# One z row through DRAM, dummies on the constant tile and a new order table in a gated linear-attention and SwiGLU kernel

## The chip, the cores and the metric

The program runs on one core of a Trainium2 chip. The metric is the device time of one execution in microseconds (us). The profile's span, from the first to the last instruction, was 1.24 to 1.39 us shorter than the device time of the same execution, so spans and times can be compared term by term.

TensorE is called PE below, VectorE DVE, ScalarE ACT, GpSimd POOL, SyncE SP.

## The reference, cut to what matters

```python
# S = 2048 tokens, D = 640, H = 32 heads of 20, F = 1728
g = sigmoid((x * gate_w).sum(-1))
# A: linear attention
phi_q = concat[softmax(q w_phi), softmax(-q w_phi)];  phi_k likewise
kv = phi_k^T v;   z = sum over tokens of phi_k          # per head
o  = (phi_q kv) / (phi_q z + 1e-6)
a  = o @ wo
# B: SwiGLU
b  = (silu(x @ w_gate) * (x @ w_up)) @ w_down
out = g * a + (1 - g) * b
```

## The kernel before

The kernel is a list of work items in a hand-tuned order. Each item issues a piece of PE work with what follows it on ACT, DVE and POOL, and every engine runs its part in that order. The letters that matter: H is a pair of dummy matmuls, put there so that PE comes to full speed earlier (the intent); X transposes a tile of x; U and V make V tiles; M makes a part of the K weights; K, S, P, E are the stages of a K tile; N finishes kv and z; Z spreads z over all partitions; Q, A, B, C, c are the stages of a Q tile (B multiplies by the spread z); F is one 128-column piece of gate and up; O is a third of the head outputs of 512 tokens; D is a tile of the output. I cuts the ring of PSUM pairs from four to three, because two banks are then held for kv; N gives the fourth back.

```python
    def next_pair():                      # the least recently used pair of PSUM banks
        return used([r for r in ring["lru"] if r < ring["n"] and r not in held][0])

    def warm():                           # H: `ones` is filled by DVE at the start
        pr = next_pair()
        mm([(bank(2 * pr, 0, P), ones[:, :], ones[:, :], True, True, False)] * NWARM)

    def kv_finish():                      # N
        ...
        reduce(zf[0:120, :], zt[0:120, :, :])
        tt("dve", dz[0:120, :, :], ident[...] broadcast, zf[...] broadcast, ALU.mult)
        ...                               # six products that write kvsb

    def z_broadcast():                    # Z: ones^T dz puts every z on every partition
        pr = next_pair()
        dzf = dz[0:120, :, :].rearrange("p j c -> p (j c)")
        mm([(bank(2 * pr, 0, 480), ones[0:120, :], dzf[:, 0:480], True, True, False),
            (bank(2 * pr + 1, 0, 480), ones[0:120, :], dzf[:, 480:960], True, True, False)])
        copy("act", zb[:, 0:960]..., halves(pr, 480))
        ...                               # and a third matmul and copy for the last 360

    # the last store of the program, issued by ACT; the others by SP
    # at the end SP waits for all stores:
    for s, v in out_evs:
        sp.wait_ge(tr.sem[s], v)
```

The softmax here doesn't subtract the row's maximum and nothing guards it: scores larger than these inputs give would overflow.

## Time and profile before

| | before |
|---|---|
| device time, median of 3 (later 5) | 290.45 us (290.59) |
| span of the profiled run | 289.1 us |
| PE busy | 285.7 us, 99% |
| DVE, ACT, POOL busy | 57%, 51%, 56% |

From the page of the kernel before, the heading, its first part (busy us, share, instructions) and its fourth part (the chain that ended last, by engine and by line):

```profile
span 289.1 us, 4875 instructions
PE 285.7 (99%) x1975; PEld 174.5 (60%) x1975; DVE 165.3 (57%) x242; ACT 147.7 (51%) x252; POOL 160.6 (56%) x124
...
PE 99%; DVE 0%; issue 0%
PE ps L294 98%; PE ps L306 1%; DVE xT L318 0%; DVE osb L712 0%; DVE ones L340 0%
```

The same chain in order of time (start us, length us, what):

```profile
1.12 2.10 PE ps L294 x18
...
8.89 278.26 PE ps L294 x1914
287.15 0.02 issue
287.18 0.32 DVE osb L712
```

PE runs without a break from 8.89 to 287.15 us. What the change can win lies in the PE work itself, in the start, and in the 2.1 us from the start of the last matmul to the end of the span, which is one eviction and the landing of the last store. PE busy time alone doesn't show this, since the ends of matmuls are modelled; the starts do: matmuls of 512 columns follow each other every 216 ns, those of 320 columns every 136 (medians in this profile).

The timeline has the matmuls that the change removes and the O parts that it makes adjacent (start us, us, engine, line, operation, out<-in, form, count):

```profile
77.22 0.72 PE L294 MATMUL ps<-dz,ones 120*128 120x480 bf16 x3
...
121.07 0.62 PE L294 MATMUL ps<-phiT,kvsb 120*64 120x512 bf16 x4
121.63 1.25 PE L294 MATMUL ps<-xT,wg 128*128 128x512 bf16 x5
122.72 1.24 PE L294 MATMUL ps<-xT,wu 128*128 128x512 bf16 x5
123.89 1.06 PE L294 MATMUL ps<-phiT,kvsb 120*64 120x512 bf16 x7
```

The DMA view of the last 2.3 us, its instruction queue q14 and its issues (KB each, us from issue to landing); the second store is the program's last:

```profile
q14 instruction: 1, 0.01, 1.0%
issues: line engine op xcount, KB each, median us to landing
out_dram<-osb SPq DMA_DIRECT2D x1, 56.0 KB, 1.6
out_dram<-osb ACTq DMA_DIRECT2D x1, 24.0 KB, 1.5
```

These lines come back below: one packet of 8 KB on the instruction queue stands beside the last store. Here it began 1.18 us after the store's issue, when the last of the store's own packets had ended (1.12 us).

### The profile page before, as it was taken

Reading aid. Unit: us, or ns where it says so; the run is one execution under the profiler, and the core shown is the slowest. Engines: PE = TensorE matmul, PEld = TensorE weight load, DVE = VectorE, ACT = ScalarE, POOL = GpSimd, SP = SyncE. Lnnn points to the kernel's source line nnn. Section 1 sums busy time; section 2 is a strip of 40 time slices with the busy share of each in tenths; the row PEclk is TensorE's granted clock in tenths of the full one; section 3 lists DMA queues with packets and bytes.
Section 4 is the critical chain, followed back from the end, with each engine's and each line's share of the span. In section 5 each row is a group of like instructions: output and inputs, shape, how many; then the busy total and the mean of one; then the engine's idle time right before and its main releaser. Section 6 shows DMA issues by size and latency. Waiting matters only on the chain.

```text
span 289.1 us, 4875 instructions
## 1 busy us (share of the span) xinstructions
PE 285.7 (99%) x1975; PEld 174.5 (60%) x1975; DVE 165.3 (57%) x242; ACT 147.7 (51%) x252; POOL 160.6 (56%) x124
## 2 busy tenths in 40 slices
PE   8999999999999999999999999999999999999997
PEld 6667777757444545457765566556444447556776
DVE  1258586865599994679989562549633883000000
ACT  1368687856747536762364542624655551344112
POOL 8587979994447886746435544256258586111000
DMA  7966798000006852202440323030402005000101
GB/s 220 189 122 128 107 263 298 3 3 0 0 2 170 239 112 50 50 2 50 106 114 0 77 50 73 25 73 23 52 0 41 11 0 124 25 23 0 48 23 49
DMA packets 48777, 21.28 MB, mean 74 GB/s; under 512 B 39346, under 2 KB 48754, under 8 KB 48754
## 3 DMA queue, kind: packets, MB, share of 16 engines
q1 hardware_dynamic: 47368, 20.25, 30.7%
q10 hardware_dynamic: 1386, 0.71, 0.8%
q8 instruction: 16, 0.26, 0.4%
q14 instruction: 7, 0.06, 0.1%
HBM read 8.96 MB, written 2.62 MB: 40 GB/s over the span
## 4 chain that ended last, share of the span: by engine, by line
PE 99%; DVE 0%; issue 0%
PE ps L294 98%; PE ps L306 1%; DVE xT L318 0%; DVE osb L712 0%; DVE ones L340 0%
## 5 line engine op out<-in xcount | busy, mean ns | idle before, releaser
L322 POOL TENSOR_TENSOR hT<-hT,us 128x512 bf16<-128x512 bf16 (+1 forms) x56 | 69.0, 1239 | 77.7 <-DVE hT L326 77.5
L326 DVE SCALAR_TENSOR_TENSOR hT<-hT,ps 128x512 bf16<-128x512 bf16 (+1 forms) x56 | 38.0, 684 | 69.1 <-ACT hT L312 64.7
L294 PE MATMUL ps<-xT,wg 128*128 128x512 bf16 x260 | 64.6, 379 | 0.0
L294 PE MATMUL ps<-xT,wu 128*128 128x512 bf16 x260 | 64.6, 379 | 0.0
L294 PE MATMUL ps<-wd,hT 128*128 128x320 bf16 (+2 forms) x462 | 63.9, 295 | 0.0
L312 ACT ACTIVATE hT<-ps 128x512 bf16<-128x512 f32 (+2 forms) x60 | 35.8, 597 | 41.1 <-PE ps L294 40.8
L294 PEld LDWEIGHTS ps<-wd,hT 128*128 128x128 bf16 x462 | 44.5, 98 | 17.8
L322 POOL TENSOR_TENSOR ph<-eq,qc 128x1320 bf16<-128x1320 bf16 x16 | 39.3, 2456 | 16.2 <-DVE qc L625 12.4
L294 PE MATMUL ps<-wqk,xT 128*128 128x320 bf16 x320 | 47.7, 299 | 0.0
L294 PEld LDWEIGHTS ps<-xT,wu 128*128 128x128 bf16 x260 | 25.4, 98 | 30.7
L294 PEld LDWEIGHTS ps<-xT,wg 128*128 128x128 bf16 x260 | 25.1, 98 | 29.0 <-issue 1.3
L312 ACT ACTIVATE osb<-ps,omg 128x640 bf16<-128x640 f32 (+2 forms) x17 | 12.9, 757 | 57.9 <-PE ps L294 57.9
L322 POOL TENSOR_TENSOR ekr<-ekr,krec 128x1280 bf16<-128x1280 bf16 x16 | 37.3, 2357 | 4.8 <-DVE krec L336 4.7
L294 PEld LDWEIGHTS ps<-wqk,xT 128*128 128x128 bf16 x320 | 30.4, 98 | 13.4 <-issue 0.4
L312 ACT ACTIVATE us<-ps 128x512 bf16<-128x512 f32 (+1 forms) x56 | 33.4, 596 | 0.1
L312 ACT ACTIVATE eq<-ps 128x640 bf16<-128x640 f32 x32 | 22.3, 703 | 21.2 <-POOL ph L322 14.2
L333 DVE TENSOR_REDUCE ksum<-ekr 128x64 f32<-128x1280 bf16 x16 | 23.4, 1461 | 9.6 <-ACT ekr L312 9.6
L312 ACT ACTIVATE ekr<-ps 128x640 bf16<-128x640 f32 x32 | 22.3, 703 | 6.4 <-PE ps L294 5.9
L294 PE MATMUL ps<-wvg,xT 128*128 128x320 bf16 (+1 forms) x160 | 24.9, 302 | 0.3 <-DVE xT L318 0.3
L333 DVE TENSOR_REDUCE qz<-eq 128x64 f32<-128x1280 bf16 x16 | 23.6, 1478 | 2.2 <-ACT eq L312 2.2
L294 PE MATMUL ps<-wog,oT 128*128 128x320 bf16 (+2 forms) x165 | 24.7, 294 | 0.0
L333 DVE TENSOR_REDUCE qw<-ez 128x64 f32<-128x1280 bf16 x16 | 23.7, 1479 | 0.2
(73 smaller groups left out, 190.3 us busy)
## 6 DMA issues: line engine op xcount, KB each, us to landing
out_dram<-osb SPq DMA_DIRECT2D x15, 160.0 KB, 1.8
wd<-in_B_w_down_dram SPq DMA_DIRECT2D x1, 2080.0 KB, 9.7
wg<-in_B_w_gate_dram SPq DMA_DIRECT2D x1, 1040.0 KB, 10.0
wu<-in_B_w_up_dram SPq DMA_DIRECT2D x1, 1040.0 KB, 12.2
wg<-in_B_w_gate_dram SPq DMA_DIRECT2D x1, 800.0 KB, 5.5
wu<-in_B_w_up_dram SPq DMA_DIRECT2D x1, 800.0 KB, 7.7
wog<-in_A_wo_dram SPq DMA_DIRECT2D x2, 375.0 KB, 7.0
wvg<-in_A_wqkv_dram SPq DMA_DIRECT2D x4, 160.0 KB, 3.7
```

Source lines behind the costliest of these rows:

```text
L294: last = pe.matmul(o, lhsT=l, rhs=r, start=st, stop=sp_, skip_group_check=sk)
L306: last = pe.transpose(o, i, ident[0:k, 0:k])
L312: return run("act", lambda: act.activation(o, i, func, scale=scale), rd, [o])
L322: return run(e, lambda: eo.tensor_tensor(o, a, b, op), [a, b], [o])
L326: return run("dve", lambda: dve.scalar_tensor_tensor(out=o, in0=a, scalar=s, in1=b, op0=op0, op1=op1), rd, [o])
L333: return run("dve", lambda: dve.tensor_reduce(o, i, AX.X, ALU.add), [i], [o])
```

## The change

The intent: take the three z matmuls off PE (z becomes a row by one PE transpose, goes to DRAM and comes back spread over the partitions by a DMA), start the dummies without waiting for a filled tile, run the O parts of one block next to each other, and lay out the order anew around the longer way of z. The diff, cut to its core:

```diff
-H0 H1 H2 H3 H4 H5 H6 H7 H8 G X0 H9 H10 H11 U0.0 X1 U0.1 U1.0 ...
-... V3 Y i4 F0.0 F0.1 M0 V4 M2 M1 M3 i3 M4 K0 K1 S0 I P0 ...
-... E12 E13 E14 E15 Q2 Q0 Q1 N J T F0.13 F1.8 A0 F1.7 Z B1 B0 F1.12 C0 c0 B2 F1.5 F1.2 F0.8 A2 C2 L Q3 F0.4 ...
-... F0.12 B4 O0.1 F0.3 O0.0 C4 O0.2 B6 F1.4 c4 B5 Q7 ...
+H0 H1 H2 H3 H4 H5 H6 H7 H8 H12 G X0 H9 H10 H11 U0.0 X1 H13 U0.1 U1.0 ...
+... V3 Y F0.1 M1 i3 M0 I F0.0 M2 V4 M3 M4 K0 K1 S0 V6 ...
+... E13 F1.11 E14 Q1 E15 Q0 Q2 N A0 Z J F0.9 F0.13 F1.13 A1 B1 B0 F1.2 F1.3 F1.0 C0 ...
+... F0.4 A5 B4 Q6 F0.11 C4 O0.0 O0.2 c4 B5 A6 O0.1 C5 c5 Q7 Q8 B6 C6 c6 D0.1 ...
@@ on-chip tiles
-    ones = sb("ones", [P, P], BF16)
-    dz = sb("dz", [P, NCH, 120], BF16)
+    zh = sb("zh", [P, P], BF16)
+    zr = sb("zr", [P, 120], BF16)
-    memset("dve", ones[:, :], 1.0)
@@ def fills(i)
+            memset("pool", zh[:, NCH:P], 0.0)
@@ def warm()
-        mm([(bank(2 * pr, 0, P), ones[:, :], ones[:, :], True, True, False)] * NWARM)
+        c = nc.const_aps.tensor(1.0, [P, P], BF16)
+        ...  # NWARM matmuls with c as both operands
@@ def kv_finish()
-        tt("dve", dz[...], ident[...], zf[...], ALU.mult)
+        copy("dve", zh[0:120, 0:NCH], zf[0:120, :])
@@ Z
-    def z_broadcast(): ...
+    zrow = nc.dram_tensor("zrow", (NCH, 120), BF16, kind="Internal").ap()
+    def z_row():
+        pr = next_pair()
+        o = bankbf(2 * pr, 120)
+        transposes([(o, zh[0:120, :])], 120)
+        copy("act", zr[0:NCH, :], o[0:NCH, :])
+        dma("sp", zrow, zr[0:NCH, :])
+        dma("sp", zb[:, :], bass.AP(zrow.tensor, zrow.offset, [[0, P], [1, FP]]))
```

More of the change, by code (lines that the diff above doesn't have):

```diff
@@ L36 @@
 ORDER = """
-H0 H1 H2 H3 H4 H5 H6 H7 H8 G X0 H9 H10 H11 U0.0 X1 U0.1 U1.0 U1.1 X2 U0.2 U1.2 U2.0 U2.1 X3 U2.2
-U0.3 U1.3 U2.3 U0.4 U1.4 U2.4 V3 Y i4 F0.0 F0.1 M0 V4 M2 M1 M3 i3 M4 K0 K1 S0 I P0 K3 S1 K2 V6 V8
-E0 K4 S3 S2 V5 P1 P3 P2 E1 V11 S4 P4 K5 V7 E2 K6 E3 K7 S5 S6 S7 E4 R1 P5 K8 R2 P6 E5 S8 V9 K9 P7
-E6 V10 P8 K10 S9 R3 E7 K11 E8 S10 R0 K12 P9 R4 P10 S11 E9 V14 K13 P11 S12 E10 K14 P12 E11 S13 P13
-K15 S14 V12 V13 P14 S15 P15 F0.6 F0.2 V15 E12 E13 E14 E15 Q2 Q0 Q1 N J T F0.13 F1.8 A0 F1.7 Z B1
-B0 F1.12 C0 c0 B2 F1.5 F1.2 F0.8 A2 C2 L Q3 F0.4 c2 A1 F1.13 F0.5 F1.6 C1 F1.1 Q5 F1.0 A3 F1.10 B3
-c1 Q4 C3 F1.9 c3 F0.7 F0.10 Q6 F0.11 F1.3 A4 F0.9 F0.12 B4 O0.1 F0.3 O0.0 C4 O0.2 B6 F1.4 c4 B5 Q7
-A6 A5 C5 c5 C6 D0.1 A7 c6 B7 C7 Q8 D0.2 D0.0 c7 A8 Q9 A9 B9 C9 Q10 F1.11 B8 c9 D0.3 C8 O1.1 B10
-A10 O1.0 O1.2 F2.6 c8 Q12 F2.3 Q11 F2.7 F2.1 B11 D1.0 C10 c10 F2.2 D1.1 A11 F2.4 Q13 C11 c11 F2.5
-A12 B13 D1.3 F2.13 F2.0 B12 C12 D1.2 A13 O2.0 O2.1 O2.2 C13 Q14 A14 c12 F2.10 F3.11 F2.12 F3.9
-F3.6 F2.9 B14 c13 Q15 F2.11 F2.8 F3.7 C14 F3.10 F3.0 B15 F3.13 A15 F3.3 F3.4 c14 C15 c15 F3.12
-F3.8 D2.2 D2.3 F3.1 F3.2 D2.0 O3.0 O3.1 O3.2 F3.5 D2.1 D3.1 D3.0 D3.2 D3.3
+H0 H1 H2 H3 H4 H5 H6 H7 H8 H12 G X0 H9 H10 H11 U0.0 X1 H13 U0.1 U1.0 U1.1 X2 U0.2 U1.2 U2.0 U2.1
+X3 U2.2 U0.3 U1.3 U2.3 U0.4 U1.4 U2.4 V3 Y F0.1 M1 i3 M0 I F0.0 M2 V4 M3 M4 K0 K1 S0 V6 V5 S1 P0
+K3 K2 P1 E0 V9 K4 E1 S3 V7 P3 K5 S2 V8 V10 S4 P2 P4 E2 R0 E3 K6 S5 P5 S6 i4 E4 V14 K7 K8 P6 V15 S7
+R2 E5 K9 S8 P7 R1 E6 K10 S9 V12 P8 E7 P9 K11 S10 P10 F0.8 R3 F1.10 E8 E9 K12 E10 S11 S12 K14 S14
+V11 K13 P11 P12 E11 K15 P14 R4 S13 P13 F1.9 S15 P15 E12 V13 T F1.8 E13 F1.11 E14 Q1 E15 Q0 Q2 N A0
+Z J F0.9 F0.13 F1.13 A1 B1 B0 F1.2 F1.3 F1.0 C0 c0 B2 F0.3 F1.12 A2 C2 F0.2 F0.7 F0.12 L c2 Q3 A3
+F1.6 C1 B3 c1 F1.4 F1.1 F1.7 F0.6 Q4 C3 c3 A4 F1.5 F0.5 F0.10 Q5 F0.4 A5 B4 Q6 F0.11 C4 O0.0 O0.2
+c4 B5 A6 O0.1 C5 c5 Q7 Q8 B6 C6 c6 D0.1 B7 Q9 D0.3 A7 C7 c7 D0.0 B9 A9 Q10 B8 D0.2 C9 O1.2 O1.0 c9
+O1.1 A8 F2.3 F2.8 Q12 F2.10 A12 F2.4 F2.13 A10 C8 c8 F2.6 F2.7 Q11 F2.0 B11 A11 B10 C11 c11 D1.0
+C10 B12 c10 F2.9 D1.2 D1.3 D1.1 O2.2 C12 O2.1 O2.0 F3.13 F2.12 F3.10 c12 F3.11 Q15 F2.1 F2.11 Q13
+Q14 F2.2 A15 F3.1 A14 B13 F3.6 F3.7 B14 A13 F3.0 F3.8 C13 F2.5 C14 c14 F3.3 c13 F3.12 B15 F3.9
+D2.3 C15 c15 F3.2 F3.5 D2.2 D2.0 O3.2 O3.0 O3.1 F3.4 D2.1 D3.2 D3.1 D3.0 D3.3
 """
@@ L466, in warm, with fn @@
         pr = next_pair()
-        mm([(bank(2 * pr, 0, P), ones[:, :], ones[:, :], True, True, False)] * NWARM)
+        c = nc.const_aps.tensor(1.0, [P, P], BF16)
+        def fn():
+            for _ in range(NWARM):
+                last = pe.matmul(bank(2 * pr, 0, P), lhsT=c, rhs=c, start=True, stop=True)
+            return last
+        run("pe", fn, [], [bank(2 * pr, 0, P)])
     def v_pairs(t, pr):
@@ L568, in kv_finish @@
         reduce(zf[0:120, :], zt[0:120, :, :])
-        tt("dve", dz[0:120, :, :], ident[0:120, 0:120].unsqueeze(1).to_broadcast([120, NCH, 120]),
-           zf[0:120, :].unsqueeze(2).to_broadcast([120, NCH, 120]), ALU.mult)
+        copy("dve", zh[0:120, 0:NCH], zf[0:120, :])
         for bk, j0, j1 in ((KV0, 0, 8), (KV0 + 1, 8, NCH)):
@@ L576, in kv_finish @@
                    hmask[0:120, hh:hh + 1].unsqueeze(1).to_broadcast([120, n, DH]), ALU.mult)
-    def z_broadcast():
+    zrow = nc.dram_tensor("zrow", (NCH, 120), BF16, kind="Internal").ap()
+    tr.reg(zrow.tensor, "sbuf", 1 << 20)
+    def z_row():
         pr = next_pair()
-        dzf = dz[0:120, :, :].rearrange("p j c -> p (j c)")
-        mm([(bank(2 * pr, 0, 480), ones[0:120, :], dzf[:, 0:480], True, True, False),
-            (bank(2 * pr + 1, 0, 480), ones[0:120, :], dzf[:, 480:960], True, True, False)])
-        copy("act", zb[:, 0:960].rearrange("p (b c) -> p b c", b=2), halves(pr, 480))
-        pr = next_pair()
-        mm([(bank(2 * pr, 0, 360), ones[0:120, :], dzf[:, 960:FP], True, True, False)])
-        copy("act", zb[:, 960:FP], bank(2 * pr, 0, 360))
+        o = bankbf(2 * pr, 120)
[3 more added lines that the diff above has]
+        dma("sp", zb[:, :], bass.AP(zrow.tensor, zrow.offset, [[0, P], [1, FP]]))
     def gates():
@@ L730, in _build @@
         "f": lambda i: load_ffn(FCUT[i], FCUT[i + 1]), "L": load_late_weights, "T": tail_weights, "J": gates,
-        "Y": w_blocks, "I": kv_begin, "N": kv_end, "Z": z_broadcast,
+        "Y": w_blocks, "I": kv_begin, "N": kv_end, "Z": z_row,
         "Q": qtile, "A": qsum, "B": qden, "C": qscale, "c": qmul,
```

## The prediction

> **What bounds the kernel.** TensorE. The page gives PE 285.7 of 289.1 us busy; the chain of waits is 99% PE, 278 us of it unbroken from 8.9 us. Busy is not peak, so I compared matmul starts in the timeline: 512-column matmuls start every 216 ns[...]. Another 1.1 us lies before the first matmul, 2 us after the last. DVE (57%), ACT (51%) and POOL (56%) have slack. No reordering can win 2% (5.8 us).
>
> **On PE.**
> - z: three matmuls against `ones` (0.56 us from start to next start) go, one 120-column transpose (0.05 us) comes: -0.5 us.
> - O parts: entering and leaving a run of O matmuls costs about 95 ns each. The first block has two runs (121.1 and 123.9 us), now one: -0.2 us.
> - Dummies: without the memset (0.90 to 1.07 us) the first can start 0.2 us earlier, but the first transposes wait for x0, landing at 3.17 us. H12 fills this time, H13 sits in the wait for the second xT copy. 0 to -0.25 us[...].
>
> **Off PE.** DVE loses the 1.53 us dz product, ACT 1.34 us of zb evictions. The z row takes two dependent DMAs: about 2 us to DRAM (stores here land in 1.77 us[...])[...]. With the copy behind the exponentials of three Q items, zb should land 7 to 8 us after the transpose (before: 2.5 from the z matmuls). Three F items, A0 and A1 lie between; DVE should wait 0 to 2 us at the first zb product. That costs nothing: four PSUM pairs hold PE's next items.
>
> **The new order.** I walked it by hand with the trace's durations (F 2.16 us, K/Q/V 1.36, E 0.34; POOL: kmul 2.36, hT 1.15, ph 2.43). In the K phase POOL gains 3.6 us (fill of ph) and 2 us (hT of F0.8, F1.10), but PE gains the F time too, and each E item finds its kmul 1 to 2 us early. M1 starts near 14.1 us, after its wT (11.6 us). phiT lands 5 us ahead of the first O block. So I expect no PE stall over 0.3 us after 9 us: the order re-covers a PE that was covered.
>
> **Time.** 290.45 - 0.5 - 0.2 - 0.1 = 289.65 us; range 288.8 to 290.8, the upper side for an overlooked stall. Faster by over 2%: 0.01; within 2%: 0.96; slower: 0.03.
>
> **What would show it.** Right: span near 288.3 us, chain still 98 to 99% PE; z matmuls replaced by one transpose; one O run per block; the DVE wait on zb now released by a DMA, up to 2 us, no PE gap beside it; first matmul near 0.93 us and first transposes of x still near 3.2 us. Wrong: PE gaps near 40 to 75 us (E items waiting for POOL), at the first M items, or after the z row; or the x transposes moving.
>
> **What would make it wrong.** The zb chain taking over 12 us, so that DVE holds all four PSUM pairs; POOL falling behind in the K phase[...].

The sum under "Time": 290.45 - 0.5 (z) - 0.2 (O parts) - 0.1 (dummies) = 289.65 us. The 0.1 was the estimate within the 0 to -0.25 us. The 7 to 8 us for zb stand as the estimate. From the trace of before: the medians of the time from each matmul's start to the next, taken by shape and tiles, add up to 283.9 of the 285.8 us between the first and the last start, and of the other 2.0 us 1.6 lie before 8.9 us.

## The result

The changed kernel took 291.62 us (median of 5, 291.38 to 291.81), the kernel before 290.59 us (median of 5, 289.97 to 290.79). The ratio is 1.0038, 95% interval 1.0023 to 1.0052: 1.1 us slower where 0.8 us faster was expected.

The page of the changed kernel has the same shape, but its chain is no longer all PE:

```profile
span 290.4 us, 4891 instructions
PE 284.9 (98%) x1977; PEld 174.6 (60%) x1977; DVE 162.9 (56%) x241; ACT 147.5 (51%) x251; POOL 160.4 (55%) x125
...
PE 96%; DMA 2%; DVE 1%; SPq 0%; ACT 0%; issue 0%
```

Its chain in order of time:

```profile
1.73 4.95 DMA wvg<-in_A_wqkv_dram
...
6.72 1.00 PE ps L294 x6
...
17.87 0.61 ACT hT L312
18.48 0.02 issue
18.50 0.69 DVE hT L326
19.19 0.74 DVE wqk L318
19.93 0.14 issue
20.07 59.32 PE ps L294 x562
...
129.46 0.08 issue
129.54 158.03 PE ps L294 x1020
287.57 0.02 issue
287.59 0.32 DVE osb L718
```

The PE stream now has three interruptions: a wait for weights at 6.72 us, one for a DVE copy (line L318, `wqk`) at 20.07 us, a short one at 129.54 us. The timeline shows that the two intended savings on PE took place: one transpose in place of three matmuls, and one run of O parts:

```profile
79.22 0.22 PE L306 MATMUL ps<-ident,zh 120*128 120x120 bf16 x1
...
127.97 1.49 PE L294 MATMUL ps<-phiT,kvsb 120*64 120x512 bf16 x11
129.54 2.88 PE L294 MATMUL ps<-wqk,xT 128*128 128x320 bf16 x20
```

The DMA view of the last 3.2 us:

```profile
q14 instruction: 1, 0.01, 1.0%
issues: line engine op xcount, KB each, median us to landing
out_dram<-osb SPq DMA_DIRECT2D x1, 56.0 KB, 1.6
out_dram<-osb ACTq DMA_DIRECT2D x1, 24.0 KB, 2.4
```

The last store takes 2.4 us to land, 0.9 more than before, with the same bytes.

One pair of profiles is a thin basis. Both kernels were therefore profiled a second time, and every later kernel gives one profile more. The table splits each span, by matmul starts in the trace, into the start (to the first F matmul), the stream (first F to the last matmul's start; the stretch to the first K matmul is given apart) and the end.

| kernel | start | F to K | stream | end | last store lands after | SP instructions |
|---|---|---|---|---|---|---|
| before | 12.03 | 7.43 | 274.90 | 2.13 | 1.49 | 82 |
| b_again | 13.99 | 7.43 | 274.91 | 2.09 | 1.45 | 82 |
| b_const | 11.58 | 7.43 | 274.91 | 2.13 | 1.49 | 82 |
| b_wait2 | 12.05 | 7.43 | 274.92 | 2.11 | 1.47 | 82 |
| b_order | 12.11 | 7.66 | 275.81 | 2.09 | 1.45 | 82 |
| b_sp2 | 12.67 | 7.43 | 274.90 | 3.02 | 2.38 | 84 |
| b_dma2 | 11.96 | 7.43 | 274.91 | 2.97 | 2.16 | 84 |
| after | 12.72 | 7.66 | 274.63 | 3.02 | 2.38 | 84 |
| a_again | 12.14 | 7.66 | 274.63 | 2.91 | 2.27 | 84 |
| a_ones | 11.99 | 7.66 | 274.89 | 2.89 | 2.26 | 84 |
| a_wait12 | 12.37 | 7.66 | 274.62 | 2.93 | 2.30 | 84 |
| a_oldorder | 12.27 | 7.43 | 277.31 | 2.92 | 2.28 | 84 |
| a_f12 | 12.19 | 7.65 | 274.62 | 2.09 | 1.45 | 82 |
| a_latei | 11.88 | 7.27 | 274.41 | 3.08 | 2.44 | 84 |
| a_best | 11.52 | 7.26 | 274.41 | 2.18 | 1.54 | 82 |

Where the code of the stream is the same, the stream repeats to 0.02 us, but for a_ones (below). The end is 2.09 to 2.18 us in one group of kernels and 2.89 to 3.08 us in the other, with nothing between. The start differs from run to run. (a_best3, the last kernel, is not in the table: start 14.29, F to K 7.27, stream 278.93, end 2.17, last store 1.52, 82 SP instructions.) So from the changed code comes -0.28 us of stream and +0.85 us of end (means of the two profiles each), together +0.57 us. Neither the waits of the PE view alone nor one pair of spans would have told this.

### The profile page after: what moved, and what is told of

It is laid out like the page before. It is cut to its first block, busy times and chain, and to the rows that moved or that the text cites. A ratio compares the mean times of both kernels' runs of the same rounds, so it can differ in the third digit from the quotient of the medians.

```text
span 290.4 us, 4891 instructions
## 1 busy us (share of the span) xinstructions
PE 284.9 (98%) x1977; PEld 174.6 (60%) x1977; DVE 162.9 (56%) x241; ACT 147.5 (51%) x251; POOL 160.4 (55%) x125
## 4 chain that ended last, share of the span: by engine, by line
PE 96%; DMA 2%; DVE 1%; SPq 0%; ACT 0%; issue 0%
PE ps L294 96%; DMA wvg<-in_A_wqkv_dram 2%; SPq L348 0%; DVE wqk L318 0%; DVE hT L326 0%; PE ps L306 0%; ACT hT L312 0%; DVE osb L718 0%
## 5 line engine op out<-in xcount | busy, mean ns | idle before, releaser
L322 POOL TENSOR_TENSOR hT<-hT,us 128x512 bf16<-128x512 bf16 (+1 forms) x56 | 65.6, 1181 | 68.0 <-DVE hT L326 67.8
L322 POOL TENSOR_TENSOR ph<-eq,qc 128x1320 bf16<-128x1320 bf16 x16 | 42.3, 2645 | 26.1 <-DVE qc L631 24.0
L312 ACT ACTIVATE eq<-ps 128x640 bf16<-128x640 f32 x32 | 22.4, 704 | 17.3 <-POOL ph L322 10.4
L333 DVE TENSOR_REDUCE ksum<-ekr 128x64 f32<-128x1280 bf16 x16 | 23.5, 1470 | 10.4 <-ACT ekr L312 10.4
```

What stands on the lines that cost most here:

```text
L312: return run("act", lambda: act.activation(o, i, func, scale=scale), rd, [o])
L322: return run(e, lambda: eo.tensor_tensor(o, a, b, op), [a, b], [o])
L333: return run("dve", lambda: dve.tensor_reduce(o, i, AX.X, ALU.add), [i], [o])
```

## The experiments

### Is the slow start the change's?

The first suspicion was the start: in the first profile of the changed kernel the second chunk of the V weights landed at 6.68 us instead of 5.17, and U0.1 waited 1.4 us for it. Theory 1: the change does this. Theory 2: landing times are chance. Four runs: both kernels unchanged, before with the constant-tile dummies alone (`b_const`), and after with the filled tile back (`a_ones`).

```diff
# b_const, against before (ones and its memset stay, for z)
-        mm([(bank(2 * pr, 0, P), ones[:, :], ones[:, :], True, True, False)] * NWARM)
+        c = nc.const_aps.tensor(1.0, [P, P], BF16)
+        ...  # as in the changed kernel
# a_ones, against after: the same the other way round, with
+    ones = sb("ones", [P, P], BF16)
+    memset("dve", ones[:, :], 1.0)
```

> The kernel before, unchanged, for a second profile. Theory 1 (the changed kernel's start is slower by itself): the second w chunk of the V weights lands again near 5.2 us, the second x transposes are followed by U items at 6.3 us, the last store lands 1.5 us after its issue; time 290.5 us. Theory 2 (landing times of the first loads and of the last store are chance of each execution): the chunk lands anywhere between 5 and 7 us and the last store takes 1.5 to 2.4 us, with the time following them.

> The changed kernel, unchanged, for a second profile. Theory 1: the second w chunk lands again near 6.7 us with a PE gap of about 1.4 us before U0.1, and the last store takes 2.4 us again; 291.6 us. Theory 2: this profile shows a landing near 5.2 us or a short last store, and then a span near 289 us, though the five times before were all 291.4 to 291.8.

> The kernel before with only the dummies reading the constant tile (the ones tile and its memset stay, for z). If the earlier and differently placed dummies disturb the first loads: U0.1 or U1.0 waits for the second w chunk near 6.7 us and the time is 0.7 us above before. If not: first matmul at 0.84 us instead of 1.12[...], time within 0.3 us of before or 0.2 faster.

> The changed kernel with the dummies reading a filled tile again, all else as changed (also puts 256 bytes per partition back, so every later tile moves). If the constant-tile dummies are the cause of the slow start: 0.7 us faster than the changed kernel, 290.9 us. If the order, the z row or chance is: 291.6 us as before it.

Measured: b_again 291.07 us (289.92 to 292.36), a_again 291.48 us (290.93 to 292.95), b_const 290.62 us, a_ones 291.13 us, beside 290.37 us for before on that chip (289.86 to 293.32). The spans of the second pair of profiles have the opposite sign of the first: before 291.0, after 289.7 us. In the timeline of PE in b_again, the kernel before, stands a wait for the same DMA as in the changed one. The first profile of the kernel before, which has no such wait:

```profile
6.30 0.72 PE L294 MATMUL ps<-wvg,xT 128*128 128x320 bf16 x4 [0.31 <-DVE xT L318]
```

The first profile of the changed kernel:

```profile
6.72 1.00 PE L294 MATMUL ps<-wvg,xT 128*128 128x320 bf16 x6 [1.40 <-DMA wvg<-in_A_wqkv_dram]
```

And b_again:

```profile
5.08 0.74 PE L306 MATMUL ps<-ident,xs 128*128 128x128 bf16 x5
6.63 1.79 PE L294 MATMUL ps<-wvg,xT 128*128 128x320 bf16 x6 [0.81 <-DMA wvg<-in_A_wqkv_dram]
```

The chunk landed at 5.2, 6.6, 5.3, 5.5, 5.5, 6.1 and 5.5 us in the seven profiles of kernels made from before, and at 6.7, 6.1, 5.4, 5.3, 5.4, 5.1, 5.2 and 5.4 in the eight of the table made from after. Theory 1 falls as far as the landings go: either code has early and late ones. The time of a_ones, 291.13 us, lies between its two expectations (290.9 and 291.6) and decides nothing. The constant tile does what it was meant to in one respect (first matmul at 0.84 us instead of 1.12), but the PE then waits for the same DMAs.

The landing is not all of the scatter. The six matmuls above take 1.79 us in b_again and 1.00 us in the changed kernel: in b_again they start 240 to 270 ns apart, in the changed kernel 135 to 147. So PE was still at about half speed in b_again. By the spacing of its matmuls (at 128 columns 107 ns before and 56 ns after in the kernel before) PE came to full speed at 4.1 to 10.0 us in the seven profiles with dummies on the filled tile (5.5 us in before, 10.0 in b_again), and at 3.9 to 10.4 us in the nine with the constant tile (4.1 us in after, 10.4 in a_best3). The two slowest starts, 13.99 us (b_again) and 14.29 us (a_best3), are the two in which PE came to full speed last. So the earlier dummies do not fix the time of full speed, and what they win, if anything, is below the scatter of the start.

(The 0.26 us by which the stream of a_ones is longer than that of after is a wait at F0.8 near 52.3 us: the last up weights landed at 52.2 us in that run, at 50.8 and 51.6 us in the two profiles of the changed kernel. The new order asks for them that early.)

### Where does the late last store come from?

In the packet records of the trace, one DMA packet of 8 KB on an instruction queue (0.46 to 0.61 us long) falls beside the last store in every profile; the expectations call it the fetch. In the kernel before it began 1.18 us after the store's issue, when the store's own packets (0.86 to 1.12 us) were done. In the changed kernel it began 1.02 us after the issue, lasted 0.58 us, and the last of the store's packets ended only 0.1 us after it: 1.70 us after the issue. None of the store's own packets took over 24 ns; some started late. The trace shows two instruction queues, q8 with packets of 16 KB and q14, that of this packet, with packets of up to 8 KB; it does not name the engine whose instructions a packet holds. The packet lies right before the late store packets (1.59 to 1.69 us). But whose is it, and why does it lie there only in the changed kernel? Theory F: it is ScalarE's, and its place goes with ScalarE's instructions, 300 here instead of 298. Rivals: the order, the z row, the memory layout.

```diff
# b_wait2: two semaphore instructions more on ACT (four satisfied waits), before the 14th output
# a_wait12: twelve more, against after
+        if t == 13:
+            for _ in range(4):            # 24 in a_wait12
+                act.wait_ge(tr.sem["pe"], 1)
# b_order: before with the order table of after;  a_oldorder: after with the order table of before
```

> The kernel before plus two ScalarE semaphore instructions that are already satisfied (300 instructions instead of 298), placed where ScalarE waits 4 us for matmuls. Theory F (ScalarE's fetch of its next 8 KB of instructions[...] collides with that store's packets in the changed kernel because ScalarE has 300 instructions there): the fetch starts about 1.02 us after the last store's issue instead of 1.17, the store takes 2.3 us instead of 1.5, from last matmul start to the end of the span 2.9 us instead of 2.1, all else as before; about 0.8 us slower. Rival (the late last store comes from the new order, the z row or memory layout): 2.1 us at the end, no change.

> The changed kernel plus twelve satisfied ScalarE semaphore instructions (312). Theory F: the last 8 KB fetch starts 0.8 to 1 us earlier against the store's issue and is out of the way of its packets: last store 1.5 us, end 2.1 us after the last matmul start instead of 2.9; about 0.8 us faster than the changed kernel. Rival: end stays at 2.9 us.

> The new order with everything else as before (z by three matmuls, dummies on the filled tile). From the first F matmul to the last matmul start, 274.90 us in the kernel before and 274.63 in the changed one: here 275.1 if the z row is worth 0.5 us of it and the order costs 0.2 (wait at the M items 0.39 instead of 0.17, wait after the adjacent O parts eating their gain). If instead the z row brought waits of its own: below 274.6. ScalarE has 301 instructions here and SyncE as many as before: by theory F the last store is late or near to it, by the rivals z row or layout it is not.

> The changed kernel with the old order table. zb lands about 6 us after the z transpose, VectorE waits 4 to 5 us for it at the first product. Theory 1 (four PSUM pairs cover this): no PE gap over 0.1 us beside it, 274.4 us from the first F to the last matmul start, so the z row did not need the new order. Theory 2 (the order had to be redone for the longer z path): PE gaps of 1 us or more at the F and Q items after the z transpose. ScalarE has 297 instructions here and SyncE 84 as in the changed kernel: theory F says last store 1.5 us, end 2.1 us.

Measured: b_wait2 290.75, a_wait12 291.64, b_order 291.62, a_oldorder 294.68 us, beside 290.91 for before. The ends in the table: 2.11, 2.93, 2.09 and 2.92 us. Theory F falls on all four: ScalarE's count is 300, 312, 301 and 297, and the end does not follow it. The order is not it either: b_order has the new order and the short end, a_oldorder the old one and the long end. What goes with the long end is the z row, or SP's two instructions more (84 instead of 82) that issue its DMAs. Three theories remained (SP's instructions, the number of DMAs, the layout of on-chip memory), told apart by two further kernels made from before and one made from after:

```diff
# b_sp2, against before: as b_wait2, on SP (two semaphore instructions more)
+                sp.wait_ge(tr.sem["pe"], 1)
# b_dma2, against before: two tiny DMAs of SP to a spare row in DRAM, waited for by DVE
+        if t == 8:
+            for r in range(2):
+                spare.append(dma("sp", scratch[r:r + 1, :], ident[r:r + 1, :]))
+        if t == 12:
+            for s, v in spare:
+                dve.wait_ge(tr.sem[s], v)
# a_f12, against after: the last gate and up loads merged, two DMAs fewer
-    FCUT = [0, 256, 896, F_FFN]
+    FCUT = [0, 256, F_FFN]
-q4 f1 f2
+q4 f1
```

> The kernel before plus two satisfied semaphore instructions on SyncE (84 instructions, as in the changed kernel). So far the end after the last matmul start is 2.1 us in every kernel with 82 SyncE instructions and 73 DMAs' semaphores fewer by two, and 2.9 us in every kernel with the z row, whatever ScalarE's count. Theory S (SyncE's instruction count sets when the late fetch comes): the fetch starts 1.02 us after the last store's issue, that store takes 2.3 us, end 2.9 us. Theories D (number of DMAs and their semaphores) and L (memory layout): end 2.1 us, fetch 1.17 us or more after the issue.

> The kernel before plus two tiny DMAs to a spare row in DRAM, issued by SyncE at the ninth store, with semaphores of their own. SyncE has 84 instructions and the program two DMAs and two semaphores more, as with the z row; layout of the on-chip memory, z and order as before. Theories S and D: last store 2.3 us, end 2.9 us. Theory L: 1.5 and 2.1 us.

> The changed kernel with the last two gate and up weight loads merged into one each: two DMAs, two semaphores and two SyncE instructions fewer (82), the on-chip layout as in the changed kernel. Theories S and D: last store back to 1.5 us, end 2.1 us instead of 2.9, so 0.8 us faster than the changed kernel. Theory L or the z row itself: 2.9 us. The merged loads should land near 51 us, before the first F item that needs them (about 52 us); if not, a PE gap stands there.

Measured: b_sp2 291.65 us and b_dma2 291.70 us (4 runs each), a_f12 290.22 us (6 runs), beside 290.71 for before. None of the three ratios is clear of 1 (1.0014, 1.0028 and 0.9999, each interval includes 1): the start scatters too much, and the ends in the table decide. The DMA view of the end of b_sp2, in which nothing but two satisfied waits on SP was added to the kernel before:

```profile
q14 instruction: 1, 0.01, 0.9%
...
out_dram<-osb ACTq DMA_DIRECT2D x1, 24.0 KB, 2.4
```

and of a_f12, which has the z row, the new order and the changed layout, but 82 SP instructions:

```profile
q14 instruction: 1, 0.01, 0.9%
...
out_dram<-osb ACTq DMA_DIRECT2D x1, 24.0 KB, 1.5
```

This settles what the late store follows: the number of instructions on SP. Two more, DMA issues (the changed kernel, b_dma2) or semaphore instructions (b_sp2), move the last packet of the instruction queue forward, from 1.18 to 1.45 us after the store's issue (the profiles with 82) to 0.84 to 1.03 us (those with 84), into the time of the store's packets, 0.86 to 1.12 us.

The kept traces say a little more. In 14 of the 16 profiles this packet begins 1.10 to 1.13 us after the start of SP's 79th recorded instruction (1.37 and 1.39 us in b_again and b_wait2), whether SP has 82 instructions or 84. So the packet follows a place in SP's own stream, and two instructions more bring this place forward against the last store (from 0.07 us after its issue in the kernel before to 0.09 us before it in the changed one). That it holds SP's instructions is inferred from this; the records name no engine. In each of the eight profiles with 84 instructions 9 of the store's 144 packets, a sixteenth of them, start more than 1.15 us after the issue, and in the eight with 82 none does. In the changed kernel these 9 start from 1.59 to 1.69 us after the issue, and the 8 KB packet ends at 1.60. That they wait for it is a guess from these times; the records do not tell what made them late.

### The wait at the M items

The changed order lost 0.22 us between the first F and the first K matmul: a gap of 0.39 us over the spacing at M4, where before had two of together 0.17. In before the last 24 M matmuls stand in one piece, as the two waits are too short to split the view:

```profile
18.04 1.58 PE L294 MATMUL ps<-wbd,wT 128*128 128x140 bf16 x24
```

and after has them with a gap:

```profile
19.36 0.48 PE L294 MATMUL ps<-wbd,wT 128*128 128x140 bf16 x6
20.07 0.47 PE L294 MATMUL ps<-wbd,wT 128*128 128x140 bf16 x6 [0.23 <-DVE wqk L318]
```

(The idle time in brackets is less than the gap, as the ends of matmuls are modelled.) My hand walk had checked the arrival of the weights and not the PSUM pair. I stands before F0.0 in the new order, so the ring has three pairs at the M items; M4 gets the pair of M2, and M2's copy stands on DVE behind F0.0's product, as the chain of the changed kernel shows from 17.87 to 19.93 us (hT on ACT, hT on DVE, wqk on DVE).

```diff
# a_latei, against after: the ring is cut where the kernel before cut it
-... F0.1 M1 i3 M0 I F0.0 M2 V4 M3 M4 K0 K1 S0 V6 ...
+... F0.1 M1 i3 M0 F0.0 M2 V4 M3 M4 K0 K1 S0 I V6 ...
```

> The changed kernel with the ring of PSUM pairs cut from four to three only after the first K items (as in the kernel before) instead of before F0.0. If the wait of 0.39 us at the M items comes from the smaller ring (M4 has the pair of M2, whose copy stands behind F0.0's product on VectorE): the gap goes, first F to first K 7.27 us instead of 7.66, first F to last matmul start 274.24 instead of 274.63. If it comes from the order of the M items or their late weights: unchanged.

Measured: 291.18 us, beside 290.71 for before; first F to first K 7.27 us, as expected. The timeline of PE has the M matmuls in one piece, and no wait before the first K:

```profile
18.52 0.79 PE L294 MATMUL ps<-wbd,wT 128*128 128x140 bf16 x12
19.15 1.84 PE L294 MATMUL ps<-wqk,xT 128*128 128x320 bf16 x11
```

The stream is 274.41 us and not the 274.24 expected: 0.17 us of wait came back inside the first K item, which needs M3's copy (on ACT, 19.37 to 20.08 us in this profile). The smaller ring is shown to be the cause of the gap; about half of its cost can be had back this way (0.22 of 0.39 us).

### What the new order is for

The two crossed kernels b_order and a_oldorder answer this as well. With the old order the z row has little between its transpose and its use. The waits of DVE and of PE in a_oldorder (engine, what waited for: us, times, longest):

```profile
DVE ez L322 <- DMA zb<-zrow: 4.8, 1, 4.8
...
PE ps L294 <- DVE hT L326: 2.5, 1, 2.5
```

DVE stands 4.8 us before the first product with zb; the evictions of the F items queue behind it, and PE, which had gone on with the free PSUM pairs, stands still for 2.5 us until 90.14 us. My expectation that four pairs would cover this (theory 1) was wrong for the old order, and my other one (theory 2) right: a_oldorder is 3.8 us slower than before by medians. Of this its profile has 2.4 us in the stream and 0.8 in the end; four of its six runs, but not the profiled one, also had a granted clock of 0.994 and took 294.2 to 295.3 us, against 293.7 and 293.9 us for the two with 1.00. In the new order A1 and three F items stand before the product, zb lands at 85.47 us, 6.2 us after the transpose, and DVE only comes to it at 87.19 us: no wait at all. The margin is not always that wide: in a_best SP issued the broadcast 3.28 us after the small store instead of 1.24, zb landed 8.2 us after the transpose, and DVE took it up 0.02 us later, still without a gap on PE. Conversely the new order does not suit the old z: in b_order the z matmuls come right behind the Q items, and PE waits for DVE there:

```profile
79.27 0.73 PE L294 MATMUL ps<-dz,ones 120*128 120x480 bf16 x3 [0.51 <-DVE kvsb L322]
```

The releaser is the kvsb product: the least recently used pair is the one that kv held, and its last reader is that product. The z matmuls start 0.67 us late against the spacing. That is why the stream, 275.81 us, met neither of my expectations for b_order (275.1, or below 274.6). So z row and order belong together, and neither alone is a gain: 275.81 us of stream with the new order alone, 277.31 with the z row alone, 274.63 with both, 274.90 with neither.

### Both costs taken away, and the O parts

Twelve runs had been used; two more asked whether these two costs are all, and where the gain of the adjacent O parts went. Adjacent, they save 0.19 us (two borders of 95 ns), but after them PE waited 0.24 us before Q7, 0.095 of which is the border that every run of O matmuls has at its end, and 0.08 us before D0.1: 0.22 us of new waits. a_best takes the two costs away; a_best3 also moves F0.11, the item right before the block, behind it.

```diff
# a_best = a_latei and a_f12 together
# a_best3, against a_best
-... Q6 F0.11 C4 O0.0 O0.2 c4 B5 A6 O0.1 C5 c5 Q7 ...
+... Q6 C4 O0.0 O0.2 c4 B5 A6 O0.1 F0.11 C5 c5 Q7 ...
```

> The changed kernel with the two found costs taken away: the ring cut to three pairs only after the first K items, and the last two weight loads merged (SyncE 82 instructions). If these are all: first F to last matmul start 274.41 us, 2.1 us after it, so first F to end 276.5 us against 277.0 in the kernel before and 277.6 in the changed one; about 0.5 us faster than before and 1.1 faster than the changed kernel in runs whose start is equal (the start itself differs by up to 2 us between runs). If another cause is hidden: first F to end 276.8 or more.

> As a_best, with F0.11 moved from before the first block of O parts to behind it, so that the item right before the block is Q6. If the wait after the block comes from the pair of the item right before it (its eviction must fit into the 1.57 us of the three O parts): the wait of 0.24 us at Q7 goes or falls to 0.1 at F0.11, first F to last matmul start 274.1 to 274.25 us. If the O run itself costs this: 0.3 us of waits remain, 274.4.

Measured: a_best 290.00 us (289.36 to 291.44), before 290.49 us (289.93 to 290.78) on the same chip, ratio 0.9995, interval 0.9976 to 1.0014; a_best3 294.55 us. From the first F on, a_best needs 276.6 us, before 277.0 and after 277.6 us, so both costs are gone as expected, and no further one of that size is hidden from the first F on. In device time a_best is not told apart from before; it has the lowest single time of all runs, 289.36 us.

a_best3 was a bad idea: its stream is 278.93 us, where 274.1 to 274.25, or 274.4, had been expected. But it answers its question. The wait at Q7 is gone; a gap of 0.27 us over the spacing now stands at F0.11, which has the pair of Q6, now the item right before the block:

```profile
127.17 1.49 PE L294 MATMUL ps<-phiT,kvsb 120*64 120x512 bf16 x11
128.77 1.25 PE L294 MATMUL ps<-xT,wg 128*128 128x512 bf16 x5
...
136.52 0.82 PE L294 MATMUL ps<-wd,hT 128*128 128x320 bf16 x3 [2.70 <-POOL hT L322]
```

So the wait follows the item right before the block: three O parts are 1.57 us of PE work and take three of the four pairs, and the next item needs the pair of the item before them, whose eviction has not ended by then. The other blocks of O parts come right behind a D item, which is evicted by one ACT instruction of 0.79 us, and have no such wait. The third line is what I had not looked at: D0.1 reads what F0.11 makes, and moved behind the O parts F0.11 comes too close to it. PE waited 2.7 us, and the matmuls after that ran at half speed for 3.3 us (matmuls of 320 columns 267 ns apart instead of 136; after the wait of 2.5 us in a_oldorder and that of 1.4 us in the changed kernel's first profile they ran at full speed); five of its six runs had a granted clock of 0.994, and the sixth, with 1.00, was the fastest (292.95 us). The start of the profiled run was also one of the slow ones, 14.29 us.

## Why the prediction was wrong

Two steps failed. The one that took the time out of the predicted range is a term that the sum didn't have: the prediction puts "2 us after the last" matmul and carries this over unchanged, and it became 3.0 us. With the shown stream alone 290.45 - 0.28 = 290.2 us would have stood inside the range; with the end it is 291.0 us. The other is the claim that the new order would make no stall. One by one:

- What bounds the kernel, the z term (-0.5 us) and that there is no 2% in it: right. Three matmuls took 0.56 us from start to next start, the transpose takes 0.06.
- The z row off PE: right in kind, and shorter than expected. zb landed 6.2 us after the transpose in this profile (7 to 8 predicted; 6.2 to 8.2 in all profiles of kernels with the z row), and DVE did not wait. SP issued the broadcast 1.24 us after the small store, and its 338 KB landed 3.2 us after that.
- "O parts ... -0.2 us": the borders were right, the term was not. The 0.19 us came in and went out again as 0.22 us of new waits after the block, net +0.03. The larger of them, before Q7, is for the pair of the item right before the block; the 0.08 us before D0.1 was not looked into.
- "I expect no PE stall over 0.3 us after 9 us: the order re-covers a PE that was covered": this step failed. The hand walk followed weights, POOL and E items and had those right, with no gap from 21 to 79 us in the changed kernel; it did not follow which item holds the PSUM pair that the next one gets. M4 waited 0.39 us, net +0.22 us.
- "Dummies ... 0 to -0.25 us": no gain can be shown. The first matmul moved to 0.84 us (0.93 predicted) and the first transposes of x by 0.1 us, but PE did not reliably come to full speed earlier (3.9 to 10.4 us with the constant tile, 4.1 to 10.0 with the filled one), and it waits for weights that landed at 5.1 to 6.7 us, in either kind of kernel early or late.
- "2 us after the last": this step failed, by the most. It was taken as fixed, and nothing in the prediction looks at it. It grew by 0.85 us, as with two more SP instructions a packet of the instruction queue comes into the time of the last store's packets, 1.02 us after the issue instead of 1.18 in the first pair of profiles. These two issue the z row's own DMAs, so the row cost more than the 0.50 us that it saved on PE.

The parts of the stream, -0.50 (z), +0.22 (M4) and +0.03 (O), sum to -0.25 of the -0.28 us. The sum of what is shown is -0.28 + 0.85 = +0.57 us, where -0.8 had been predicted. Measured were +1.0 to +1.1 us by medians. The rest would have to lie in the start: with the later parts subtracted from every run's time, it has a mean of 12.8 us in 11 runs of the changed kernel and 12.5 us in all 55 runs of before (medians 12.8 and 12.3), with standard deviations of 0.6 and 0.8 us. In runs of the same rounds the changed kernel's start was 0.5 to 0.6 us longer both times; but in a_f12, a_latei and a_best, which have the same code up to the first F, the same difference is 0.2, -0.2 and 0.1 us. Whether the changed start is really some tenths slower stays open, and with it nearly half of the measured slowdown.

## What to carry to other kernels

When a kernel is bound by one saturated engine, a change of a fraction of a per cent is decided at the borders of the stream: profile both versions more than once, split the span into start, stream and end, and believe only what repeats. Before reordering items that share a ring of buffers, write down which item held the buffer that each item gets and which engine frees it; here three O parts in a row, 1.57 us of PE work, took three of the four pairs. Here nothing covered the last store's landing, 1.45 to 1.54 us in the profiles with 82 SP instructions and 2.16 to 2.44 us in those with 84, so look at what else the DMA queues carry in that time, also where the change has touched nothing near it.
